# Attention with a bilinear gate on one core: first projections begun on column halves, queries stored before the keys are loaded, last unit summed in one bank

## The chip, the core and the metric

The kernel runs on one core of one Trainium2 chip. The core has five engines with a queue each: TensorE (PE for its matmuls, PEld for its weight loads), VectorE (DVE), ScalarE (ACT), GpSimd (POOL) and SyncE (SP), which here issues every DMA. The engines work at the same time and wait for each other through semaphores. SBUF is the on-chip memory, PSUM the eight banks (128 x 512 float32 each) into which TensorE writes. The metric is the device time of one execution in microseconds (us). Three executions of the kernel before took 1708.01, 1708.64 and 1712.07 us; the median is 1708.64 us.

## The reference

x is 2048 tokens of 512. Its layer norm xn feeds an attention of 32 heads of 16 and a bilinear gate of width 1792; the result is x + attention * silu(gate).

```
xn = (x - mean(x)) / sqrt(var(x) + 1e-5)
q, k, v = split(xn @ wqkv)                       # 32 heads of 16
p = softmax(q @ k.T * 16 ** -0.5)
s = (p @ v).reshape(2048, 512) @ wo
g = silu(((xn @ w_gate) * (xn @ w_up)) @ w_down)
out = x + s * g
```

All arrays are float32. The kernel keeps the accuracy by splitting an operand into a high part (hi), rounded to the matmul's input format, and a low part (lo), the rest; a product is hi*hi + hi*lo + lo*hi, three matmuls.

## The kernel before, in words

The 2048 tokens are 16 tiles of 128, four tiles to a chunk (`c` 0 to 3). The 32 heads are 8 groups of four; a group with one chunk of queries is a unit, so there are 32 units, and a unit walks over the 16 key tiles in 16 rounds. In a round four matmuls `t` (line 639, one for each head) give transposed scores, ACT takes their exponentials `e` (line 641), and `pv` (line 652) multiplies them with the values; two rounds are one block of `pv`. The scores are also computed the other way round (`s`, line 617) to take row maxima on DVE (`mx`, line 619), ahead of the exponentials. The gate's matmuls (`u`, `g`, `y`) and the output projection (`z`) are put between the matmuls of the attention by a filler, so that PE always has work.

The order of the instructions on PE, ACT, DVE and POOL is the order of the program. SP's early part (to round 18) is held to the program's order too; after that a scheduler places SP's DMAs by its own estimate of when each is ready. Each queue is worked through in order, so an instruction that waits holds back all behind it on its engine.

**The start (`early`, lines 714 to 802).** Tiles of x are loaded. The tiles 0 to 3 go through one chain of layer norm: `ln_stats` on DVE for each tile, one square root on ACT for all four (`ln_root`), five small DVE operations (`ln_scale`), then `ln_apply`: tiles 1 and 3 on DVE, 0 and 2 on ACT. `ln_turn` transposes a tile on PE (`xT`) and rounds it into `fh` (hi of chunk 0; DVE for the odd, ACT for the even tiles), `ln_low` forms `fl` on DVE. Then PE projects: `k(0)` (matmuls `p`, 12 of 512 columns: four with the weights' hi `w1h`, four with their lo `w1l`, four with `fl`), `q(0)` in the same way with `w0h` and `w0l`, then values `v`. POOL makes these weights' parts in the order w1h, w1l, w0h, w0l. A table `at` says in front of which of the 252 steps that follow the later tiles are normalised, turned and scored: the first scores stand at step 66, the first that need keys of chunk 1 at step 104.

**The way through DRAM.** A projected chunk leaves PSUM as `hl` (ACT the hi, DVE or POOL the lo), is stored by SP to DRAM (`KD` for keys, `QD` for queries, line 342) and loaded again in the shape of the scores (`ks`, `qs`; `load_k`, `load_q`). SP's order at the start is: store keys 0, load keys 0, store queries 0, load queries 0, then the same for chunk 1.

**The last unit.** Unit 31 has eight blocks. Each block's `pv` goes into one of the three PSUM banks with the tag `st`, which `t` uses in turn as well; the first block is copied into an SBUF tile `acc` by ACT (line 658), the next six are added to it by DVE (line 660). The scores are finished by then, and the banks with the tag `s` have only two users left, two of the output projection's four sums.

**The end (`last_heads`, `final`, `end`).** The last block is added to `acc` in two column halves, each half is transposed, divided by its sum of exponentials and transposed back on DVE; ACT rounds it to `th`, POOL forms the rest `tl`. `final` multiplies both with the last four heads' rows of `wo` (`wrh`, `wrl`): three matmuls for each of four token tiles. `end` multiplies by the gate on DVE, adds x (tiles 0 and 2 on POOL, 1 and 3 on DVE, tile 3 in halves) and stores the tile; here tile means one of the last four, 12 to 15.

## Time and profile before

| | |
|---|---|
| median of three executions | 1708.64 us (1708.01 to 1712.07) |
| the profiled execution's own time | 1709.17 us |
| its span | 1707.0 us |
| PE busy | 1695.4 us, 99% |
| DVE busy | 1441.9 us, 84% |
| ACT busy | 1307.8 us, 77% |
| POOL busy | 872.2 us, 51% |

The profile is of one execution. A row of its timeline has the start and the length in us, the engine, the line, the operation, output<-input by the program's tile names, the shape and the count; what stands in brackets is the idle time of that engine just before and what ended it. A row with a count joins instructions that follow each other. Matmuls overlap: the recorded length of one is longer than the step to the next. SP's rows are the issue of DMAs, not their transfer.

### The profile page before, as it was taken

What the parts mean: (1) busy time and instruction counts of PE and PEld (TensorE: products, weight loads), DVE (VectorE), ACT (ScalarE), POOL (GpSimd) and SP (SyncE); (2) the same over time, 40 slices, a digit from 0 to 9 for tenths busy, and PEclk for the clock granted to TensorE, in tenths of its full rate; (3) what the DMA queues carried; (4) which work ended last, traced back from release to release, by engine and by line L of the source; (5) the groups of instructions that cost most, each with busy time, mean ns of one, the idle gap of its engine ahead of it and who ended that gap; (6) DMA issues with size and microseconds to landing.
All of it is one profiled execution on the core that took longest, in us unless ns stands there. A gap on an engine that the chain in (4) does not pass through costs nothing.

```text
span 1707.0 us, 34993 instructions
## 1 busy us (share of the span) xinstructions
PE 1695.4 (99%) x13570; PEld 1042.1 (61%) x13570; DVE 1441.9 (84%) x2492; ACT 1307.8 (77%) x2565; POOL 872.2 (51%) x873
## 2 busy tenths in 40 slices
PE   8999999999999999999999999999999999999998
PEld 6666656666566666666656665666666566665654
DVE  6888888888888888888888888888888888898953
ACT  6357778777787778778777887877778787777874
POOL 5315545762644647446354572663647536446650
PEclk9999999999999999999999999999999999999999
DMA  6317623620241312412115220330225112111362
GB/s 210 109 48 216 242 104 127 151 66 20 64 91 36 100 60 66 91 45 60 32 52 134 66 72 24 85 79 27 58 83 126 55 36 71 29 54 43 118 187 79
DMA packets 117379, 145.79 MB, mean 85 GB/s; under 512 B 12637, under 2 KB 74333, under 8 KB 114525
## 3 DMA queue, kind: packets, MB, share of 16 engines
q1 hardware_dynamic: 117212, 143.55, 29.3%
q8 instruction: 107, 1.75, 0.4%
q14 instruction: 60, 0.48, 0.1%
HBM read 95.94 MB, written 47.45 MB: 84 GB/s over the span
## 4 chain that ended last, share of the span: by engine, by line
PE 96%; DVE 1%; DMA 1%; issue 0%; POOL 0%; ACT 0%; SPq 0%; POOLq 0%
PE pv L652 28%; PE t L639 19%; PE s L617 12%; PE g L292 6%; PE g L296 5%; PE y L292 5%; PE y L296 5%; PE u L292 5%; PE u L296 4%; PE p L292 3%; PE v L273 2%; PE p L296 2%; PE z L292 2%; PE z L296 1%; DVE mx L619 0%
## 5 line engine op out<-in xcount | busy, mean ns | idle before, releaser
L619 DVE TENSOR_REDUCE mx<-s 128x1 f32<-128x512 f32 x2048 | 1255.0, 681 | 210.4 <-PE s L617 169.0
L641 ACT ACTIVATE e<-t 128x512 f32<-128x512 f32 x2048 | 1101.4, 601 | 96.2 <-PE pv L652 46.5
L639 PE MATMUL t<-qs,ks 50*128 50x512 f32 x2048 | 782.1, 407 | 0.0
L617 PE MATMUL s<-ks,qs 48*128 48x512 f32 x2048 | 767.7, 409 | 0.9 <-DMA ks<-KD 0.4
L63 POOL TENSOR_TENSOR acc<-acc,part 128x512 f32<-128x512 f32 x214 | 278.8, 1303 | 583.8 <-ACT part L663 583.5
L639 PEld LDWEIGHTS t<-qs,ks 50*128 50x128 f32 x2048 | 359.2, 185 | 268.4 <-issue 110.2
L652 PE MATMUL pv<-e,V 128*32 128x512 f32 x4096 | 492.5, 598 | 0.0
L617 PEld LDWEIGHTS s<-ks,qs 48*128 48x128 f32 x2048 | 351.2, 185 | 28.4 <-issue 5.7
L663 ACT ACTIVATE part<-pv 128x512 f32<-128x512 f32 x214 | 128.1, 599 | 204.2 <-PE pv L652 204.2
L652 PEld LDWEIGHTS pv<-e,V 128*32 128x32 f32 x4096 | 107.1, 109 | 242.2 <-issue 220.0
L292 PE MATMUL u<-fh,w0h 64*128 64x512 f32 x224 | 90.5, 404 | 0.0
L296 PE MATMUL g<-fh,w1h 64*128 64x512 f32 x224 | 90.4, 404 | 0.0
L296 PE MATMUL y<-dh,hh 64*128 64x512 f32 x224 | 89.5, 400 | 0.0
L292 PE MATMUL y<-dh,hh 64*128 64x512 f32 x224 | 89.1, 398 | 0.0
L296 PE MATMUL u<-fh,w0l 64*128 64x512 f32 x224 | 88.2, 394 | 0.0
L296 PE MATMUL g<-fl,w1h 64*128 64x512 f32 x224 | 88.1, 393 | 0.0
L292 PE MATMUL u<-fh,w0l 64*128 64x512 f32 x224 | 88.1, 393 | 0.0
L292 PE MATMUL g<-fl,w1h 64*128 64x512 f32 x224 | 88.0, 393 | 0.0
L296 PE MATMUL g<-fh,w1l 64*128 64x512 f32 x224 | 87.9, 392 | 0.0
L292 PE MATMUL g<-fh,w1h 64*128 64x512 f32 x224 | 87.9, 392 | 0.0
L296 PE MATMUL u<-fl,w0h 64*128 64x512 f32 x224 | 87.9, 392 | 0.0
L292 PE MATMUL y<-dl,hh 64*128 64x512 f32 x224 | 87.8, 392 | 0.0
(273 smaller groups left out, 2973.0 us busy)
## 6 DMA issues: line engine op xcount, KB each, us to landing
w1r<-in_wg_dram SPq DMA_DIRECT2D x56, 256.0 KB
w0r<-in_wu_dram SPq DMA_DIRECT2D x56, 256.0 KB
wdr<-in_wd_dram SPq DMA_DIRECT2D x56, 256.0 KB
qs<-QD SPq DMA_DIRECT2D x64, 192.0 KB
ks<-KD SPq DMA_DIRECT2D x12, 768.0 KB
KD<-hl SPq DMA_DIRECT2D x16, 512.0 KB
QD<-hl SPq DMA_DIRECT2D x16, 512.0 KB
OD<-acc SPq DMA_DIRECT2D x31, 256.0 KB
```

What stands on the lines that cost most here:

```text
L63: got = getattr(self.engine, name)(*args, **kw)
L273: nc.tensor.matmul(o, l(d), r(d), start=k == d == 0, stop=k == 2 and d == ND - 1)
L292: nc.tensor.matmul(outs[k], l[LOWER], r[LOWER], start=k == 0 and n == 0, stop=(stop or k == 0) and n == len(low) - 1, skip_group_check=k == 1)
L296: nc.tensor.matmul(outs[1 - k], l[UPPER], r[UPPER], start=k == 0 and m == 0, stop=(stop or k == 0) and m == len(high) - 1, skip_group_chec ...
L617: nc.tensor.matmul(o, QS[i][b:b + KB, pr, t * P:(t + 1) * P], k[b:b + KB, pr, kc * 512:(kc + 1) * 512], start=True, stop=True)
L619: nc.vector.tensor_reduce(MX[i][:, j, t, kc:kc + 1], o, axis=AX.X, op=OP.max)
L639: nc.tensor.matmul(o, k[b:b + KR, pr, kt * P:(kt + 1) * P], QS[i][b:b + KR, pr], start=True, stop=True)
L641: nc.scalar.activation(e, o, AF.Exp, scale=DH ** -0.5)
L652: nc.tensor.matmul(o[32 * j:32 * j + 32], V[:, kt, h0:h0 + 32], es[j], start=n == 0, stop=n == len(todo) - 1)
L663: nc.scalar.activation(part, o, AF.Copy)
```

## The change

In the start, the four tiles are normalised in two chains, tiles 0 and 1 first and 2 and 3 after them, each with its own square root and small operations; tile 1 is now normalised and rounded by ACT. When tiles 0 and 1 are turned, the first four matmuls of `k(0)` run on the columns 0 to 255 alone (tile `hf`), those of `q(0)` (tile `hx`) after tiles 3 and 2 are turned; `full` then does the columns 256 to 511 of these four and the other eight whole. POOL makes both hi parts of the weights first, and the lo parts after them. Keys 0 are loaded after queries 0 are stored. The table `at` moves statistics and normalisations of later tiles by some steps.

PE from its first instruction to the values' projection (xT is a turned tile, its number the tile's; p1 and p0, hf and hx are the key and query projections). Before:

```order
L737 MATMUL warm_199<-acc_127 128x512
L250 MATMUL xT1_227<-ident_129,ks1_135 128x128 x4
L250 MATMUL xT0_233<-ident_129,ks1_135 128x128 x4
L250 MATMUL xT3_239<-ident_129,ks1_135 128x128 x4
L250 MATMUL xT2_245<-ident_129,ks1_135 128x128 x4
L737 MATMUL warm_251<-acc_127 128x512
L273 MATMUL p1_0_0_288<-fh_151,w1h_257 128x512 x4
L273 MATMUL p1_0_0_288<-fh_151,w1l_258 128x512 x4
L273 MATMUL p1_0_0_288<-fl_155,w1h_257 128x512 x4
L273 MATMUL p0_0_0_317<-fh_151,w0h_261 128x512 x4
L273 MATMUL p0_0_0_317<-fh_151,w0l_262 128x512 x4
L273 MATMUL p0_0_0_317<-fl_155,w0h_261 128x512 x4
```

The same place on PE now:

```order
L251 MATMUL xT0_235<-ident_129,ks1_135 128x128 x4
L251 MATMUL xT1_241<-ident_129,ks1_135 128x128 x4
L748 MATMUL warm_249<-acc_127 128x512
L775 MATMUL hf_257<-fh_151,w1h_251 128x256 x4
L251 MATMUL xT3_263<-ident_129,ks1_135 128x128 x4
L251 MATMUL xT2_269<-ident_129,ks1_135 128x128 x4
L775 MATMUL hx_275<-fh_151,w0h_254 128x256 x4
L275 MATMUL hf_257<-fh_151,w1h_251 128x256 x4
L275 MATMUL hf_257<-fh_151,w1l_252 128x512 x4
L275 MATMUL hf_257<-fl_155,w1h_251 128x512 x4
L275 MATMUL hx_275<-fh_151,w0h_254 128x256 x4
L275 MATMUL hx_275<-fh_151,w0l_255 128x512 x4
```

Eight half-width matmuls stand ahead of the point at which all four tiles are turned and rounded; two turned tiles stand between them.

SP, the first stores and loads of keys and queries. Before:

```order
L63 DMA KD0_0_60<-hl_310 128x1024
L63 DMA KD0_0_60<-hl_310 128x512
L63 DMA ks0_134<-KD0_0_60 48x2x512 x2
L63 DMA QD0_0_67<-hl_341 128x1024
L63 DMA QD0_0_67<-hl_341 128x512
L63 DMA qs_346<-QD0_0_67 48x2x512 x2
```

The same place on SP now:

```order
L63 DMA KD0_0_60<-hl_329 128x1024
L63 DMA KD0_0_60<-hl_329 128x512
L63 DMA QD0_0_67<-hl_356 128x1024
L63 DMA QD0_0_67<-hl_356 128x512
L63 DMA ks0_134<-KD0_0_60 48x2x512 x2
L63 DMA qs_363<-QD0_0_67 48x2x512 x2
```

The load of keys 0 moved behind the store of queries 0; what follows stands as it did.

In the last unit all eight blocks of `pv` add up in one bank `last` with the tag `s`; the copy by ACT and the adds by DVE are gone, and `t` has the three `st` banks to itself. `last_heads` transposes straight from that bank. The hi and the lo of a head are laid side by side in the 32 rows that a head's block has (`both`, made by POOL), so one transposition on DVE and one copy on ACT serve both, and `final` needs two matmuls a tile, eight in all. For that the rows of `wrh` are copied into the unused rows beside them by four small DMAs on SP. In `end` tile 0 and tile 1 are added on POOL, tile 2 on DVE, and tile 3 in halves on DVE. The program's text stores tile 1 between the halves of tile 3.

SP, the last stores (y is the tile that holds the last four token tiles; the brackets name the engines waited for). Before:

```order
L63 DMA out_0_dram<-dl_24577 128x512 [waits DMAHW6_49,DMAHW2_49,DVE_49]
L63 DMA out_0_dram<-dl_24577 128x512 [waits DVE_49]
L63 DMA out_0_dram<-y_19450 128x512 [waits Pool_49]
L63 DMA out_0_dram<-y_19450 128x512 [waits DMAHW1_49,DVE_49]
L63 DMA out_0_dram<-y_19450 128x512 [waits Pool_49]
L63 DMA out_0_dram<-y_19450 128x256 [waits DVE_49] x2
```

The same place on SP now:

```order
L63 DMA out_0_dram<-dl_24595 128x512 [waits DMAHW6_49,DMAHW2_49,DVE_49]
L63 DMA out_0_dram<-dl_24595 128x512 [waits DVE_49]
L63 DMA out_0_dram<-y_19468 128x512 [waits Pool_49]
L63 DMA out_0_dram<-y_19468 128x512 [waits DMAHW5_49,Pool_49]
L63 DMA out_0_dram<-y_19468 128x512 [waits DVE_49]
L63 DMA out_0_dram<-y_19468 128x256 [waits DVE_49] x2
```

As built, the stores stand in the order tile 0, 1, 2, then the halves of 3: the scheduler has put tile 1's, which waits for POOL, ahead of tile 2's and of both halves of tile 3's.

The diff, cut to its core:

```diff
@@ split_raw @@
-    def split_raw(name, raw, after=None):
         hi, lo = [wtile(name + n) for n in "hl"]
         pool.tensor_copy(hi, raw)
-        low = pool.tensor_tensor(lo, raw, hi, op=OP.subtract)
-        if after is not None:
+        def rest():
+            low = pool.tensor_tensor(lo, raw, hi, op=OP.subtract)
             tc.add_manual_dep(low.ins, after.ins.name, BEHIND, reason="keeps the port free for the layer norm")
-        return hi, lo
+        return (hi, lo), rest
@@ full @@
+            part = slice(256 if begun and k == 0 else 0, 512)
             for d in range(ND):
-                nc.tensor.matmul(o, l(d), r(d), start=k == d == 0, stop=k == 2 and d == ND - 1)
+                nc.tensor.matmul(o[:, part], l(d), r(d)[:, part], start=k == d == 0 and not begun, stop=k == 2 and d == ND - 1,
+                                 skip_group_check=begun)
@@ end @@
-            pool.tensor_tensor(yt, yt, xt, op=OP.add)
-        dma(out[tt * P:(tt + 1) * P], yt)
+        (nc.vector if t == 2 else pool).tensor_tensor(yt, yt, xt, op=OP.add)
+        if t != 1:
+            dma(out[tt * P:(tt + 1) * P], yt)
@@ ending @@
+        for j in range(0, P, 32):
+            dmar(wrh[j + DH:j + 32], wrh[j:j + DH])
...
+        def final(t):
+            for n, r in enumerate((wrh, wrl)):
+                nc.tensor.matmul(banks[t], fst["t"][:, t * P:(t + 1) * P], r, start=False, stop=n == 1,
+                                 skip_group_check=True)
@@ block @@
-        o = psum("st", f"pv{i}")
+        whole = i == NU - 1
+        if whole and todo[0][1] == 0:
+            fst["last"] = psum("s", "last")
+        o = fst["last"] if whole else psum("st", f"pv{i}")
@@ last_heads @@
-            nc.vector.tensor_tensor(acc[:, c], o[:, c], acc[:, c], op=OP.add)
-            nc.vector.transpose(flat, acc[:, c])
+            nc.vector.transpose(tr[:, b].rearrange(flat), o[:, c])
             nc.vector.reciprocal(rc[:, b], tr[:, b, DH:DH + 1])
             nc.vector.tensor_tensor(tr[:, b, 0:DH], tr[:, b, 0:DH], rc[:, b].to_broadcast([P, 8, DH]), op=OP.mult)
-            nc.vector.transpose(acc[:, c], flat)
-            nc.scalar.activation(th[:, c], acc[:, c], AF.Copy)
-            pool.tensor_tensor(tl[:, c], acc[:, c], th[:, c], op=OP.subtract)
+            pool.tensor_copy(both[:, b, 0:DH], tr[:, b, 0:DH])
+            pool.tensor_tensor(both[:, b, DH:32], tr[:, b, 0:DH], both[:, b, 0:DH], op=OP.subtract)
+        for h in range(2):
+            c, b = slice(256 * h, 256 * h + 256), slice(8 * h, 8 * h + 8)
+            nc.vector.transpose(back[:, c], both[:, b].rearrange(flat).bitcast(F32))
+            nc.scalar.activation(fst["t"][:, c], back[:, c], AF.Copy)
@@ early @@
-        first = (0, 1, 2, 3)
-        ln_open(first)
-        for tt in first:
-            ln_stats(tt)
-        ln_root(first)
-        ln_scale(first)
-        port = ln_apply(1)
...
+        first = (0, 1), (2, 3)
...
+        ln_root(first[0])
+        ln_scale(first[0])
+        ln_apply(0)
+        ln_apply(1)
+        ln_stats(2)
+        ln_stats(3)
+        ln_root(first[1])
+        ln_scale(first[1])
+        ln_turn(0)
+        ln_turn(1)
+        port = ln_apply(3)
+        ln_apply(2)
         warm(1)
...
+        def first_half(w, tag):
+            half[tag] = o = psum(tag, f"h{tag}")
+            for d in range(ND):
+                nc.tensor.matmul(o[:, 0:256], w[0][:, d], xh[0][:, d, 0:256], start=d == 0, stop=False,
+                                 skip_group_check=True)
+        first_half(wk, "f")
+        ln_low(0)
+        ln_turn(3)
+        ln_turn(2)
+        first_half(wq, "x")
...
         def q(c):
-            yield from qk_proj(wq, 0, 0, c, "f" if c else "x")
+            yield from qk_proj(wq, 0, 0, c, "f" if c else "x", None if c else half["x"])
+            if not c:
+                load_k(0, [c])
             load_q(c)
...
-        for tts, n, root, scale in ((tuple(range(4, 8)), 0, 13, 25), (tuple(range(8, NT)), 16, 52, 53)):
+        for tts, n, root, scale in ((tuple(range(4, 8)), 0, 13, 16), (tuple(range(8, NT)), 16, 52, 53)):
```

More of the change, by code (lines that the diff above doesn't have):

```diff
@@ L305, in qk_weights, with qk_proj @@
         return split(f"w{which}", wqkv[:, c0:c0 + P])
-    def qk_proj(w, m, which, c, tag):
+    def qk_proj(w, m, which, c, tag, o=None):
         wh, wl = w
-        o = psum(tag, f"p{which}_{m}_{c}")
+        begun = o is not None
+        o = o if begun else psum(tag, f"p{which}_{m}_{c}")
         hi, lo = [lambda d, w=w: w[:, d] for w in (wh, wl)]
-        yield from full(o, ((hi, lambda d: xh[c][:, d]), (lo, lambda d: xh[c][:, d]), (hi, lambda d: xl[c][:, d])))
+        yield from full(o, ((hi, lambda d: xh[c][:, d]), (lo, lambda d: xh[c][:, d]), (hi, lambda d: xl[c][:, d])), begun)
         hl = qp.tile([P, 2, D], F32R, name="hl", bufs=HBUFS)
@@ L569, in ending @@
             yield
-        for todo in (0, 1), (2, 3):
-            final(todo, (0, 1))
-            final(todo, (2,))
+        for t in range(4):
+            final(t)
+        for t in range(4):
+            end(NC - 1, t, banks[t], fst["y"][:, t], xr[:, t])
     NU = NG * NC
@@ L652, in block @@
                 nc.tensor.matmul(o[32 * j:32 * j + 32], V[:, kt, h0:h0 + 32], es[j],
-                                 start=n == 0, stop=n == len(todo) - 1)
-        if todo[-1][1] == NT - 1 and i == NU - 1:
-            last_heads(o)
+                                 start=(kt if whole else n) == 0, stop=kt == NT - 1 if whole else n == len(todo) - 1,
+                                 skip_group_check=whole)
+        if whole:
+            if todo[-1][1] == NT - 1:
+                last_heads(o)
         elif todo[0][1] == 0:
@@ L760, in k @@
         def k(c):
-            yield from qk_proj(wk, 0, 1, c, "f")
-            load_k(0, [c])
+            yield from qk_proj(wk, 0, 1, c, "f", None if c else half["f"])
+            if c:
+                load_k(0, [c])
         def q(c):
-            yield from qk_proj(wq, 0, 0, c, "f" if c else "x")
+            yield from qk_proj(wq, 0, 0, c, "f" if c else "x", None if c else half["x"])
+            if not c:
+                load_k(0, [c])
             load_q(c)
```

61 lines of the change are left out of this document (28 added, 33 removed).

## The prediction, made before the changed kernel was run

> **What bounds the kernel now.** I read the page first: busy time, then the share of PE.
>
> ```profile
> span 1707.0 us, 34993 instructions
> PE 1695.4 (99%) x13570; PEld 1042.1 (61%) x13570; DVE 1441.9 (84%) x2492; ACT 1307.8 (77%) x2565; POOL 872.2 (51%) x873
> ```
>
> PE is busy for 99% of the span, so a change counts where PE waits or works for nothing: at the start, in the last unit, and behind the last matmul. What is won at the start is kept to the end, because the stream of matmuls behind it is the same. The profiled execution took 1709.17 us, 2.2 us more than its span; it lies 0.53 us above the median of 1708.64 us.
>
> The timeline of the start comes next.
>
> ```profile
> 4.96 0.18 DVE L205 BATCH_NORM_AGGREGATE mv<-st 128x2 f32<-128x6 f32 x1
> 5.90 0.69 DVE L204 BATCH_NORM_STATS2 st<-ks 128x6 f32<-128x512 f32 x1 [0.76 <-DMA ks<-in_x_dram]
> 7.38 0.61 POOL L63 CAST w1h<-w1r 128x512 fp32r<-128x512 f32 x1 [5.19 <-DMA w1r<-in_wqkv_dram]
> 7.64 0.30 ACT L208 ACTIVATE r<-mv,eps 128x4 f32<-128x4 f32 x1 [5.41 <-DVE mv L205]
> 7.97 0.18 DVE L214 RECIPROCAL r<-r 128x4 f32<-128x4 f32 x1 [0.36 <-ACT r L208]
> 8.97 1.52 ACT L235 ACTIVATE ks<-ks,mr,e 128x512 f32<-128x512 f32 x2 [1.03 <-DVE mr L220]
> 8.97 1.00 DVE L234 TENSOR_SCALAR ks<-ks,e,mr 128x512 f32<-128x512 f32 x2
> 9.66 1.94 PE L250 MATMUL xT<-ident,ks 128*128 128x128 f32 x16 [2.70 <-DVE ks L234]
> 11.63 0.60 ACT L260 ACTIVATE fh<-xT 128x512 fp32r<-128x512 f32 x1 [0.27 <-PE xT L250]
> 11.80 2.47 DVE L265 TENSOR_TENSOR fl<-xT,fh 128x512 fp32r<-128x512 f32 x4
> 12.33 1.16 PE L273 MATMUL p<-fh,w1h 128*128 128x512 f32 x4
> 18.11 2.03 PE L273 MATMUL v<-e,fh 128*128 128x512 f32 x8
> ```
>
> Statistics of four tiles, a square root (7.64), five small operations (7.97 to 8.97, 1.0 us), normalising, 16 transpositions, rounding: only at 12.33 does PE begin the key projection, and the values follow at 18.11. The last row gives the step of a 512-column matmul: (2.03 - 0.40)/7 = 0.23 us, where 0.40 is the recorded length of one. The 16 transpositions have a step of 1.94/16 = 0.12.
>
> The next rows show PE waiting again, and the way through DRAM.
>
> ```profile
> 18.08 0.81 SPq L63 DMA_DIRECT2D KD<-hl  x2
> 21.38 0.80 SPq L63 DMA_DIRECT2D ks<-KD  x2
> 22.01 0.66 PE L250 MATMUL xT<-ident,ks 128*128 128x128 f32 x4 [0.47 <-ACT ks L235]
> 22.28 0.86 SPq L63 DMA_DIRECT2D QD<-hl  x2
> 27.41 0.79 SPq L63 DMA_DIRECT2D qs<-QD  x2
> 30.56 0.47 PE L617 MATMUL s<-ks,qs 48*128 48x512 f32 x1
> 31.29 0.71 PE L617 MATMUL s<-ks,qs 48*128 48x512 f32 x3 [0.26 <-DMA qs<-QD]
> 35.73 0.59 ACT L313 ACTIVATE hl<-p 128x512 fp32r<-128x512 f32 x1
> 38.49 0.81 SPq L63 DMA_DIRECT2D KD<-hl  x2
> 45.81 0.46 PE L617 MATMUL s<-ks,qs 48*128 48x512 f32 x1
> 46.71 0.70 PE L617 MATMUL s<-ks,qs 48*128 48x512 f32 x3 [0.43 <-DMA ks<-KD]
> ```
>
> PE waits three times: at 22.01 for tile 4 (ACT's normalising), at 31.29 for the queries, at 46.71 for the keys of chunk 1. A store lands 3.3 us (18.08 to 21.38) or 5.1 us (22.28 to 27.41, with the keys' load beside it) after its issue, a load is used 3.9 us (27.41 to 31.29) after its own; for keys of chunk 1 store and load take 8.2 us together (38.49 to 46.71).
>
> **The start, step by step.** *First chain.* Tile 1's statistics end at 5.14; square root to 5.5, five small operations to 6.5. The first chain's root no longer waits for tile 2, which arrives at 5.90. ACT then normalises tiles 0 and 1 (1.52) to 8.0. *Second chain.* DVE does the statistics of tiles 2 and 3 behind the small operations, 2 x (0.69 + 0.18) at most, to 8.2; root to 8.5, small operations to 9.5; tile 3 on DVE (1.00/2) to 10.0, tile 2 on ACT to 10.3. The added root and five operations (1.3 us) so lie beside ACT's work on the first two tiles, which ACT rounds from 8.5 to 9.6.
>
> *Half-width matmuls.* They start at 9.7, once tile 1 is rounded; w1h is there (7.38 + 0.61), w0h is made next. No row shows a 256-column matmul. The bounds are the transposition's 0.12 (128 columns with a weight load each) and 0.23; half of 0.23 is 0.12, and the transpositions show that a weight load fits into such a step, so I take 0.12. Then: hf to 10.2, two turned tiles (8 x 0.12) to 11.1, hx to 11.6. ACT rounds tile 2 (0.60) from 11.3 to 11.9; the other halves begin at 12.0: 4 x 0.12 + 4 x 0.23 to 13.4. fl is ready: DVE has one low part before tile 3's rounding and three (0.60 each, from 2.47/4) after it, to 13.2. Keys end at 14.3, queries 0.48 + 1.84 later at 16.6, against 18.11: **1.5 us**. POOL's lo parts, moved behind w0h, start after 10.0 and are needed at 12.5 and 14.8.
>
> *Tile 4.* DVE's statistics of tiles 4 to 7 now start at 13.2 and end at 16.4, hl of the keys 17.0, small operations 18.0 (moved ahead of the queries' hl), ACT's tile 4 at 18.8. PE wants it at 19.9 (1.5 and the wait before 22.01), so the wait goes: 0.47 printed, and since a record ends 0.17 after the next matmul could have begun (0.40 - 0.23), **0.64 us**.
>
> *Queries in front of keys on SP.* Store of keys at 17.0, of queries at 18.65 (hl behind the small operations, 0.6), landed by 23.8 even at 5.1; their load is used by 27.7. The keys' load, which the store is now ahead of, is issued between 20.3 and 22.1 and lands by 26.0. PE comes to the first scores at 30.56 - 1.5 - 0.64 = 28.4. Both are early by 0.7 us or more. The wait was 0.73 from 30.56 to 31.29 less one score's 0.21: **0.52 us**.
>
> *Keys of chunk 1.* ACT made their hl at 35.73, behind four normalisations (0.76 each, from 8.97's row). Two of the four now stand behind it (1.5 us), and the rest comes some 2.1 us earlier, as PE does: hl near 32.1, store 2.8 later as before, at 34.9, use at 43.1. PE is there at 45.81 - 2.14 - 0.52 + 0.21 = 43.4. The wait of 0.90 - 0.23 goes: **0.67 us**, with only 0.3 us to spare. Late next are tiles 10 and 11, whose normalising moved: ACT ends tile 11's at 35.5, when PE wants it; I take nothing for that and keep 0.3.
>
> Sum of the start: 1.5 + 0.64 + 0.52 + 0.67 = **3.3 us**, between 2.0 and 3.6.
>
> **The last unit.** The waits of the window 1640 to 1697 and the first matmuls behind a block:
>
> ```profile
> 1684.06 3.81 ACT L641 ACTIVATE e<-t 128x512 f32<-128x512 f32 x7 [0.70 <-PE t L639]
> 1684.10 0.39 PE L296 MATMUL z<-fl,hl 64*128 64x512 f32 x1
> 1684.41 0.50 PE L639 MATMUL t<-qs,ks 50*128 50x512 f32 x1
> 1684.75 0.39 PE L292 MATMUL z<-fh,dh 64*128 64x512 f32 x1
> PEld t L639 <- DVE acc L660: 2.5, 7, 0.4
> ```
>
> The third `t` behind a block waits until DVE has read the block's bank. From 1684.10 to 1684.75 two steps take 0.65 instead of 0.46: 0.19 lost, most of it because no weights are loaded ahead during a wait. Of the seven waits listed two belong to unit 30; with the one for ACT's copy of the first block six go: 6 x 0.19 = **1.1 us**. Above, the idle time as printed gives 6 x 0.35 = 2.1. Below, nothing, if `t` then waits for ACT at the same place; ACT's seven exponentials take 3.81 us and it sat idle for 0.70 before them, so I stay near the row. DVE's six adds and ACT's copy are off the path. The four copies of `wrh` rows in SP's queue stand ahead of loads for chunk 2's output that are used only in the unit's last blocks: nothing.
>
> **The end.**
>
> ```profile
> 1653.27 2.14 DVE L492 TENSOR_TENSOR dl<-dl 128x512 f32<-128x512 f32 x2
> 1653.79 1.07 POOL L63 CAST hl<-w1r 128x512 fp32r<-128x512 f32 x1
> 1678.31 1.28 DVE L492 TENSOR_TENSOR hh<-hh 128x512 f32<-128x512 f32 x2
> 1694.95 0.42 DVE L699 TENSOR_TENSOR acc<-pv,acc 128x256 f32<-128x256 f32 x1 [3.44 <-PE pv L652]
> 1698.74 1.28 PE L561 MATMUL z<-hl,g 128*128 128x512 f32 x4
> 1699.17 0.69 DVE L484 TENSOR_TENSOR y<-z,y 128x512 f32<-128x512 f32 x1 [0.38 <-PE z L561]
> 1701.87 1.26 POOL L63 TENSOR_TENSOR y<-y,hh 128x512 f32<-128x512 f32 x1 [0.56 <-DVE y L484]
> 1703.09 0.42 DVE L480 TENSOR_TENSOR y<-z,hh 128x256 f32<-128x256 f32 x1
> L63 SPq DMA_DIRECT2D out_dram<-y x5: 332/377/472, 1701.3 to 1704.0; - x5
> GB/s 0 0 0 0 0 0 0 0 0 0 72 338 389 399 369 399 379 277 0 31 348 358 420 307 343 338 343 133 0 0 0 0 0 0 0 0 0 0 0 0
> ```
>
> `last_heads` now: per half transposition, reciprocal, product on DVE, 1.05 us each from 1694.95; POOL's rounding and rest of 128 columns, 0.7 between 0.5 (the rows' 0.61 and 1.26 for 512 scaled down) and 1.9 (not scaled); back through DVE and ACT: first half at 1698.0, second at 1698.8. PE does tile 0's two matmuls at 1698.05; DVE's first product follows 0.43 behind the last of them, as 1699.17 follows 1698.74: at 1698.7, **0.47 us earlier**. DVE's work behind it is the same eight operations as before (4.3 us, 1699.17 to 1703.51).
>
> But tile 2's add on DVE reads two SBUF tiles while POOL adds tiles 0 and 1. Two such adds took 2.14 us at 1653.27 with POOL at work and 1.28 at 1678.31 with POOL idle; POOL's rounding took 1.07 instead of 0.61. So DVE loses 0.4 and ends at 1703.4, and POOL's second add, done at 1702.0 without that, ends about 1702.65.
>
> As SP stands, the stores of tile 2 and of tile 3's halves wait behind tile 1's, which waits for that add. With 0.38 for an issue: 1702.65, 1703.05, 1703.4, 1703.8; before, the last began at 1704.0. The bytes say the other sign: at some 350 GB/s (the slices at full rate) 768 KB behind 1702.65 end 0.2 us later than 512 KB behind 1703.13 (1701.87 + 1.26) did. I take **0**, between 0.8 earlier (no collision) and 0.6 later.
>
> The Trainium skill's page "SBUF — State Buffer", section "SBUF: two separate sides", says that the shared port pair is an exclusive lock which the loser waits for during the whole instruction. By it tile 2's add could wait for all of a POOL add (1.26), and the end would come 0.4 us later than I take; the two rows above show 0.43 an add, and I go by them.
>
> **Sum.** 3.3 + 1.1 + 0 = 4.4 us: 1709.17 becomes 1704.8 for the profiled execution, and 1708.64 becomes **1704.2 us** for the median, 0.26% less. What a measurement of this kernel can tell from no change is about 0.3%, 5.1 us: the line is at 1703.5.
>
> **Rivals.**
> - *The end pays.* If DVE and POOL do not collide, tile 1's store goes at 1702.0 and the end is 0.8 earlier; with the start at 3.6: 1708.64 - 5.5 = 1703.1. For it: at 1701.87 POOL's add ran in 1.26 beside DVE, though DVE then read a PSUM bank. Chance 0.30.
> - *Half-width matmuls cost as much as whole ones* (0.23): queries end at 17.9 and the start gains 2.0. 1705.5, chance 0.08. Against it: the transpositions' 0.12.
> - *The waits come back*: keys of chunk 1 or the first queries late after all, `t` waiting for ACT. 1.5 + 0.64 is left: 1706.5, chance 0.12. For it: 0.3 us to spare.
> - *Slower.* The mechanism is SP's order: keys 0 wait behind the queries' store, that for DVE's hl, that for five small operations, that for ACT's root, that for the statistics of tiles 4 to 7, loaded from 5.89 on. Whatever delays that chain now delays keys and queries together. Each us beyond 0.7 costs one; it decides at 0.7 + 4.4 = 5.1 us, and 10.2 us make the kernel 0.3% slower, near 1714. No row speaks for so much. Chance 0.13, for this and what I don't see.
>
> The Trainium skill's page "TensorE: Matmul & The Clock Gate", section "LDWEIGHTS (loading the stationary operand)", gives columns/1.2 ns, 107 ns for 128 columns. Were that not hidden behind the matmul, a half would be an estimated 0.22 us and the second rival true; the trace's step of 0.23 for 512 columns with a load each speaks for hiding.
>
> **How the numbers follow.** Forecast 0.37 (its own range 1703.3 to 1705.4, a quarter of it below 1703.5), rivals 0.30, 0.08, 0.12, 0.13. Faster: 0.30 + 0.10 = 0.40. Same: 0.27 + 0.08 + 0.12 = 0.47. Slower: 0.13. The range runs from 1702.4 (start 3.6, last unit 1.8, end 0.8) to 1706.8 (waits back, end 0.3 later) and leaves out the slower rival and the edges.
>
> **What the changed profile would show.** The second half of hf near 12.0 and the values near 16.6; no idle ahead of tile 4, the first scores near 28.4 and step 104 near 43 without a wait; no wait of `t` for DVE in the last 45 us; tile 2's add on DVE near 1.1 us instead of 0.65; last store's issue about 9 us after the last `pv` as before (1704.0 - 1694.8). I am wrong if scores wait again, if a half-width step is 0.2, or if the shift at step 104 is lost later.

## The result, and the profile after

The changed kernel takes 1704.66 us (median of nine executions, 1704.20 to 1705.57) against 1708.64 us, a ratio of 0.9974 with a 95% interval of 0.9964 to 0.9985. The forecast was 1704.2 us in a range of 1702.4 to 1706.8. The profiled execution took 1704.54 us.

The page of the changed kernel, first lines: span, then busy time by engine.

```profile
span 1702.8 us, 35005 instructions
PE 1693.3 (99%) x13574; PEld 1042.9 (61%) x13574; DVE 1437.5 (84%) x2487; ACT 1307.8 (77%) x2567; POOL 873.5 (51%) x875
```

PE worked 2.1 us less than before (1695.4) and waited 2.1 us less (span less PE: 9.5 after 11.6). The timeline of the start follows, with the marks that the prediction named (lines 251, 275, 621, 643 answer to 250, 273, 617, 639 of before).

```profile
9.76 0.71 PE L775 MATMUL hf<-fh,w1h 128*128 128x256 f32 x4
10.30 1.06 PE L251 MATMUL xT<-ident,ks 128*128 128x128 f32 x8
12.05 0.74 PE L275 MATMUL hf<-fh,w1h 128*128 128x256 f32 x4 [0.21 <-ACT fh L261]
16.86 2.03 PE L275 MATMUL v<-e,fh 128*128 128x512 f32 x8
17.26 0.80 SPq L63 DMA_DIRECT2D KD<-hl  x2
19.16 0.82 SPq L63 DMA_DIRECT2D QD<-hl  x2
20.12 0.60 PE L251 MATMUL xT<-ident,ks 128*128 128x128 f32 x4
28.51 0.73 PE L621 MATMUL s<-ks,qs 48*128 48x512 f32 x4
30.38 0.66 PE L251 MATMUL xT<-ident,V 128*128 128x128 f32 x4
31.57 0.73 PE L275 MATMUL p<-xh,w0h 128*128 128x512 f32 x2
32.90 0.72 PE L621 MATMUL s<-ks,qs 48*128 48x512 f32 x4
35.14 0.81 SPq L63 DMA_DIRECT2D KD<-hl  x2
43.53 0.73 PE L621 MATMUL s<-ks,qs 48*128 48x512 f32 x4
96.12 0.50 PE L643 MATMUL t<-qs,ks 50*128 50x512 f32 x1
```

The second half of `hf` starts at 12.05, the values at 16.86 (before 18.11); tile 4, the first scores and the scores of step 104 have no bracket, so PE didn't wait there. The lead over the kernel before can be followed row by row: 1.25 us at the values, 1.89 at tile 4 (22.01), 2.57 at the second of the first scores (31.29 against 28.51 + 0.21), 2.20 at the next scores (before they began at 35.10), 2.97 at step 104 (46.71 against 43.53 + 0.21), 3.16 at the first `t`, which was at 99.28. It grows at each wait that went, and falls once, between 28.5 and 32.9. There two small waits are new, for tile 8 and ahead of the queries' projection; PE loses 0.16 and 0.22 us in them. From the start of the two matmuls ahead to what follows it takes 0.63 us (29.75 to 30.38) and 0.78 us (30.79 to 31.57), and in the kernel before 0.47 us (32.49 to 32.96) and 0.56 us (33.31 to 33.87) at the same places.

The last block of the last two units, before and after (`last` is the new bank), shows what the last unit gave:

```profile
1645.94 1.92 PE L652 MATMUL pv<-e,V 128*32 128x512 f32 x16
1692.91 1.92 PE L652 MATMUL pv<-e,V 128*32 128x512 f32 x16
```

```profile
1642.75 1.92 PE L659 MATMUL pv<-e,V 128*32 128x512 f32 x16
1688.67 1.92 PE L659 MATMUL last<-e,V 128*32 128x512 f32 x16
```

The lead is 3.19 us at the end of unit 30 and 4.24 at the last `pv`: the last unit gave 1.05 us. The wait of `t` for DVE's sums, seven times and 2.5 us in all in the kernel before, is left once, in unit 30:

```profile
PEld t L643 <- DVE acc L669: 0.3, 1, 0.3
```

The end:

```profile
1694.42 1.89 DVE L489 TENSOR_TENSOR y<-z,y 128x512 f32<-128x512 f32 x3 [0.25 <-PE z L567]
1695.19 2.96 POOL L63 TENSOR_TENSOR y<-y,hh 128x512 f32<-128x512 f32 x2 [1.50 <-DVE y L489]
1696.34 0.69 DVE L493 TENSOR_TENSOR y<-y,hh 128x512 f32<-128x512 f32 x1
1696.50 3.58 SPq L63 DMA_DIRECT2D out_dram<-y  x5
```

The bandwidth by windows (start:end, length, PE, PEld, DVE, ACT, POOL busy with counts, PE clock, DMA share, GB/s):

```profile
1698.50:1699.00 0.50, 0.00 (x0) 0.00 (x0) 0.26 (x1) 0.00 (x0) 0.00 (x0) 0.68 0.05 12
1701.00:1701.50 0.50, 0.00 (x0) 0.00 (x0) 0.00 (x0) 0.00 (x0) 0.00 (x0) 0.50 0.57 193
```

DVE's first product follows the last `pv` by 5.75 us, 0.51 less than before (1699.17 - 1692.91 = 6.26). But from the last `pv` to the end of the span it takes 14.1 us in both kernels. The gain of VectorE is lost between its work and the stores: the DMA engines are nearly idle ahead of 1699.0 (12 GB/s) and then have 768 KB to move, which keeps them busy past 1701.0.

### The profile page after: what moved, and what is told of

It is laid out like the page before. It is cut to its first block, busy times and chain, and to the rows that moved or that the text cites. A ratio compares the mean times of both kernels' runs of the same rounds, so it can differ in the third digit from the quotient of the medians.

```text
span 1702.8 us, 35005 instructions
## 1 busy us (share of the span) xinstructions
PE 1693.3 (99%) x13574; PEld 1042.9 (61%) x13574; DVE 1437.5 (84%) x2487; ACT 1307.8 (77%) x2567; POOL 873.5 (51%) x875
## 4 chain that ended last, share of the span: by engine, by line
PE 98%; DVE 1%; ACT 0%; DMA 0%; POOL 0%; issue 0%; ACTq 0%
PE pv L659 27%; PE t L643 19%; PE s L621 12%; PE g L295 6%; PE y L295 5%; PE u L295 5%; PE g L299 5%; PE y L299 4%; PE u L299 3%; PE p L295 3%; PE v L275 2%; PE z L295 2%; PE p L299 2%; PE last L659 1%; PE z L299 1%; PE p L275 1%
## 5 line engine op out<-in xcount | busy, mean ns | idle before, releaser
L659 PE MATMUL pv<-e,V 128*32 128x512 f32 x3968 | 477.1, 598 | 0.0
L299 PE MATMUL g<-fh,w1h 64*128 64x512 f32 x224 | 90.6, 404 | 0.0
L295 PE MATMUL g<-fh,w1l 64*128 64x512 f32 x224 | 87.9, 392 | 0.0
L299 PE MATMUL g<-fh,w1l 64*128 64x512 f32 x224 | 87.9, 392 | 0.0
L295 PE MATMUL y<-dh,hl 64*128 64x512 f32 x224 | 87.8, 392 | 0.0
```

The source lines that it names most:

```text
L295: nc.tensor.matmul(outs[k], l[LOWER], r[LOWER], start=k == 0 and n == 0, stop=(stop or k == 0) and n == len(low) - 1, skip_group_check=k == 1)
L299: nc.tensor.matmul(outs[1 - k], l[UPPER], r[UPPER], start=k == 0 and m == 0, stop=(stop or k == 0) and m == len(high) - 1, skip_group_chec ...
L659: nc.tensor.matmul(o[32 * j:32 * j + 32], V[:, kt, h0:h0 + 32], es[j], start=(kt if whole else n) == 0, stop=kt == NT - 1 if whole else n ...
```

## The experiments

Each kernel was timed in alternation with the kernel before, which took 1708.99 us beside the first set (`start_only`, `tail_only`, `one_bank_old_end`, `stores_in_order`), 1709.01 beside the second (`changed_again`, `keys_first`, `no_halves`, `norm_earlier`) and 1709.15 beside the third (`keys_first_fed`, `no_halves_fed`, `old_table`, `add2_on_gpsimd`). Differences below are against these, or against the changed kernel as timed in the second set, 1704.91 us.

**The two ends of the change apart.** `start_only` is the changed kernel with the old functions `block`, `last_heads`, `final` and `end`, and without the copies of `wrh` rows:

```diff
-        o = fst["last"] if whole else psum("st", f"pv{i}")
+        o = psum("st", f"pv{i}")
...
-        for t in range(4):
-            final(t)
+        for todo in (0, 1), (2, 3):
+            final(todo, (0, 1))
+            final(todo, (2,))
```

`tail_only` has only these from the change, and the old `early`, `full` and `qk_proj`:

```diff
-        first = (0, 1), (2, 3)
+        first = (0, 1, 2, 3)
...
-        first_half(wk, "f")
```

> The start of the change alone (two chains of layer norm, column halves, the table of steps, the queries' store in front of the keys' load), with the last unit and the end of the kernel before. By my theory the start's shift of 3.2 us (the first t at 96.12 us against 99.28 us in the two traces) is kept to the end and nothing else moves: 1708.64 - 3.2 = 1705.4 us, within 0.4. The rival, that part of the shift comes from or is lost in the last unit, gives less than 1705.0 or more than 1706.0.

> The last unit and the end of the change alone, with the start of the kernel before. By my theory the last unit gives 1.05 us (3.19 of lead at its start, 4.24 at its last pv in the trace of after) and the end nothing: 1707.6 us, within 0.4, and the two halves of the change add up to 4.25 us. The rival, that the two do not add, shows as a sum of both gains that differs from 4.0 by more than 0.6.

`start_only` took 1705.87 us, 3.12 less than the kernel before (ratio 0.9980, 0.9972 to 0.9989), `tail_only` 1707.79 us, 1.20 less (0.9994, 0.9985 to 1.0003). The sum, 4.32 us, agrees with the change's 4.1 in the second set: within this noise the two halves add up. The interval of `tail_only` includes no change at all, so what the last unit is worth is better read from the traces: there it gave 0.99 us in `tail_only` and 1.05 us in the next run, as in the changed kernel.

**One bank, old end.** The kernel before, and in it:

```diff
-        o = psum("st", f"pv{i}")
+        o = fst["last"] if whole else psum("st", f"pv{i}")
...
-            nc.vector.tensor_tensor(acc[:, c], o[:, c], acc[:, c], op=OP.add)
-            nc.vector.transpose(flat, acc[:, c])
+            nc.vector.transpose(flat, o[:, c])
```

> The kernel before with only the last unit's sums kept in one bank; the rounding of the last heads, the six matmuls, the products and the stores stay those of before, less the addition of the last block (0.42 us a half), which the bank makes needless. My theory: the last unit gives its 1.05 us here too, and the end is shorter by 0.4 to 0.8, as the addition lay on its path and the stores of before wait for nothing else: 1707.0 us (1706.7 to 1707.3), so 0.4 to 0.8 better than the last unit and the end of the change together. The rival, that the rewritten end is worth as much as the addition it drops, or more: 1707.6 or above.

It took 1707.44 us, 1.55 less than before (0.9990, 0.9981 to 0.9999). That lies between theory and rival. The trace shows more:

```profile
1691.18 1.92 PE L655 MATMUL last<-e,V 128*32 128x512 f32 x16
1695.66 0.39 PE L292 MATMUL z<-fh,w0l 64*128 64x512 f32 x1
1697.01 1.08 PE L561 MATMUL z<-hl,g 128*128 128x512 f32 x4
1697.44 0.69 DVE L484 TENSOR_TENSOR y<-z,y 128x512 f32<-128x512 f32 x1 [0.81 <-PE z L561]
```

From the last `pv` to the first product it takes 6.26 us, exactly as before: in the old end the addition was not on the path. PE is still busy with the open sums of chunk 3 until about 1695.9, and tile 0's third and last final matmul is the fifth behind them, at 1697.01; the product follows 0.43 later. So the dropped addition alone buys nothing, and my expectation of 0.4 to 0.8 at the end fell. In the changed kernel tile 0 is through after two matmuls, and its product comes 0.51 us earlier, although the first of the two starts later behind the last `pv` (1693.66 - 1688.67 = 4.99 against 1695.97 - 1691.18 = 4.79). It waits for ACT's rounding there and no longer for PE, so the addition could count in the new end; no run has the new end with the addition. The 0.35 us between this kernel and `tail_only` are there in the traces before the last unit, at the end of unit 30 (1645.26 against 1645.59), up to which both run the program of before. The first `t` came at 98.54 and 98.80 us, against 99.28 in the trace of the kernel before, so the unchanged start itself varies by that much.

**The stores in the written order.** The changed kernel, and ahead of the last stores:

```diff
         while "t" not in fst:
             yield
+        Tied.on = True
```

which holds SP to the order of the program.

> The changed kernel with the last five stores issued in the order in which they are written in the code: tiles 0, 2, first half of 3, tile 1, second half of 3. My theory: the end's gain on VectorE (0.54 us) is lost because the stores of tile 2 and of tile 3's first half, whose data are there at 1697.03 and 1697.83 us, stand behind tile 1's, which waits for GpSimd's second addition until 1698.15; the DMA engines are idle for the us before 1699.0. In the new order 384 KB less move after 1699.0 and the last issue comes right behind the last operation at 1698.76 instead of 1699.6: 0.5 to 0.8 us faster than after, 1703.9 to 1704.2 us. The rival, that the end hangs on the last store's own latency behind VectorE's last operation or on the rate of the DMA engines, whatever the order: within 0.2 us of after.

```profile
1688.88 1.92 PE L660 MATMUL last<-e,V 128*32 128x512 f32 x16
1696.71 2.70 SPq L63 DMA_DIRECT2D out_dram<-y  x5
1698.50:1699.00 0.50, 0.00 (x0) 0.00 (x0) 0.44 (x2) 0.00 (x0) 0.00 (x0) 1.00 0.98 356
1700.50:1701.00 0.50, 0.00 (x0) 0.00 (x0) 0.00 (x0) 0.00 (x0) 0.00 (x0) 0.87 0.08 23
```

It took 1703.96 us, 5.03 less than the kernel before (0.9969, 0.9958 to 0.9981), where the change gave 4.1 in the second set. By the two medians of the changed kernel (1704.66 and 1704.91) that is 0.7 to 0.9 us better, at the upper end of the theory or a little over it. The issues of the five stores span 2.70 instead of 3.58 us, in the window from 1698.5 the bytes move at 356 GB/s, where the changed kernel had 12, they are through by 1701.0 (23 GB/s in the last window), and the span ends 13.1 us behind the last `pv` (1702.0 - 1688.88) instead of 14.1. The order in SP's queue ate the end's gain.

**Tile 2's addition on GpSimd**, in addition to the ordered stores (one execution, 1705.75 us):

```diff
-        (nc.vector if t == 2 else pool).tensor_tensor(yt, yt, xt, op=OP.add)
+        pool.tensor_tensor(yt, yt, xt, op=OP.add)
```

> The changed kernel with the stores in the written order and tile 2's last addition on GpSimd, behind those of tiles 0 and 1, instead of on VectorE. My theory: GpSimd's second addition took 1.72 us because VectorE's addition of two SBUF tiles (0.69 us) ran beside it; without that each of the three takes 1.26 to 1.30. VectorE ends 0.6 us earlier, at about 1697.9 us, but tile 2's store waits for GpSimd until 1699.2 (1695.4 + 3 x 1.28), so the span ends 0.2 to 0.6 us later than with VectorE's addition. The rival, that the store of tile 0, which reads SBUF meanwhile, slows the second addition: 1.7 us again.

The groups by line, for the changed kernel and then for this one:

```profile
L63 POOL TENSOR_TENSOR y<-y,hh 128x512 f32<-128x512 f32 x2 | 3.0, 1500 | 1.5 <-DVE y L489 1.5
```

```profile
L63 POOL TENSOR_TENSOR y<-y,hh 128x512 f32<-128x512 f32 x3 | 3.7, 1266 | 1.5 <-DVE y L489 1.5
1697.05 4.24 SPq L63 DMA_DIRECT2D out_dram<-y  x5
```

Three additions take 1266 ns each here; with VectorE's addition beside them two took 1500 on average, so the second took about 1.73. The collision is real, and here GpSimd pays for it, not VectorE (0.69 us in the row at 1696.34). The store of tile 0 isn't the cause. VectorE doesn't always come off free. In the run with one bank and the old end its product of 128 columns took 0.29 us for the first half and 0.80 us for the second, beside an operation of GpSimd:

```profile
1695.27 0.73 POOL L63 TENSOR_TENSOR g<-acc,g 128x256 fp32r<-128x256 f32 x1 [36.95 <-ACT g L707]
1695.35 0.80 DVE L705 TENSOR_TENSOR tr<-tr,rc 128x128 f32<-128x128 f32 x1
```

In both cases the operation that began second lost: GpSimd's second addition 0.09 us behind VectorE's (1696.43 against 1696.34), VectorE's product 0.08 us behind GpSimd's. The time I gave was too small: the span ends 14.8 us behind the last `pv` (1704.0 - 1689.22), 1.7 later than with VectorE's addition, since in the written order tile 2's store holds back all three behind it, and it now waits for the third addition.

**The changed kernel again, as a base.**

> The changed kernel itself, as the base for the kernels run beside it on the same chip: 4.0 to 4.4 us faster than before, as measured already. No theory differs here.

1704.91 us, 4.10 less than the kernel before (0.9975, 0.9965 to 0.9985).

**Keys first on SP.** The load of keys 0 back in front of the queries' store:

```diff
-            if c:
-                load_k(0, [c])
+            load_k(0, [c])
...
-            if not c:
-                load_k(0, [c])
```

> The changed kernel with SyncE's old order at the start: the load of the keys of chunk 0 back in front of the queries' store. My theory: the load waits for the keys' store to land (issue 17.26, landed by 21.15 us in the trace of after) and holds the queries' store from 19.16 to about 22.0; that lands 3.9 to 5.1 us later, the queries' load is used 3.9 us after its issue, so at 29.8 to 31.0, while PE is at the second score at 28.7: a wait of 1.1 to 2.3 us at the first scores, all of it kept to the end: 1.1 to 2.3 us slower than the changed kernel beside it. In the kernel before, the swap looked worth only its wait of 0.52 us, since PE came later there. The rival, that the new wait is 0.5 us as before or that a wait behind it is covered by it: 0 to 0.6 us slower.

It took 1709.67 us, 4.8 more than the changed kernel, and as much as the kernel before (ratio 1.000, 0.9991 to 1.0009). Theory and rival were both far too low. SP and PE:

```profile
27.62 0.80 SPq L63 DMA_DIRECT2D qs<-QD  x2
30.80 2.03 PE L621 MATMUL s<-ks,qs 48*128 48x512 f32 x4 [2.43 <-DMA qs<-QD]
38.05 0.73 PE L621 MATMUL s<-ks,qs 48*128 48x512 f32 x4
```

The wait lies just above what I forecast (1.1 to 2.3 us): the scores begin at 30.80 instead of 28.42 us, 2.38 late. But the four scores then take 2.03 us instead of 0.73, and the next scores begin 7.25 us later instead of 4.40 (28.42 to 32.82 in the run beside it). PE alone in windows (length, busy with count, granted clock, DMA share, GB/s):

```profile
26.00:28.00 2.00, 2.00 (x11) 1.00 0.04 14
31.00:32.00 1.00, 0.92 (x3) 0.50 0.00 0
37.00:38.00 1.00, 1.00 (x6) 0.81 0.00 0
```

Behind the pause the granted clock is 0.50 until about 37.4 us (the mean of 0.81 in the last window is 0.38 us at half), so for some 6.6 us of work, with no DMA traffic beside it, and that costs another 2.85 us. The first `t` is at 101.27 us, 5.23 behind the changed kernel's 96.04.

**The same, with PE kept at work through the wait.**

```diff
+            if n == 66:
+                warm(10)
```

> The kernel with the keys' load in front of the queries' store, with ten matmuls on zeros (10 x 0.23 us) put on PE ahead of the first scores, where it waited 2.7 us; their result is not used. My theory: of the 4.8 us that this order cost, the wait itself is 2.4 to 2.7, and the rest is TensorE's granted clock, which stood at 0.50 from 31 to 37.2 us behind the wait. With PE fed through the wait the clock stays at 1.00: 2.3 to 2.9 us slower than the changed kernel (1707.2 to 1707.8 us by 1704.9), and about 2.2 faster than without the ten matmuls. The rival, that the slow matmuls come from what runs beside them (DMA traffic, other engines' PSUM access) and not from the pause: the four scores take 2.0 us again and the time is 1709 to 1710 us.

```profile
28.36 8.74 PE L748 MATMUL warm<-acc 128*128 128x512 f32 x20
37.03 0.74 PE L621 MATMUL s<-ks,qs 48*128 48x512 f32 x4
40.85 0.73 PE L621 MATMUL s<-ks,qs 48*128 48x512 f32 x4
31.00:32.00 1.00, 1.00 (x4) 1.00 0.00 0
```

1713.17 us: the ten matmuls were mis-sized. They multiply float32 tiles, are recorded as 20, and take 8.74 us instead of the 2.3 that I worked out from the projections' 0.23; so the time says nothing on the wait. The rows behind them do: the four scores take 0.74 us, and the next scores follow in 3.82 us, not 7.25. With no pause ahead of them the same matmuls run at full clock. The granted clock is 1.00 in every window from 24 to 39 us, also between 31 and 37 us (the last line), which speaks against what goes on beside PE at that time as the cause. That, and the granted clock of 0.50 above, carry the reading that the pause is what slowed them.

**Without column halves**, two chains kept:

```diff
-        first_half(wk, "f")
+        half.update(f=None, x=None)
...
-        first_half(wq, "x")
```

> The changed kernel without the column halves: two chains of layer norm as they are, but the key and query projections begin at full width once all four tiles are turned. My theory: eight 256-column matmuls (8 x 0.115 = 0.92 us) that ran while PE waited for tiles 2 and 3 come on top behind 12.0 us; nothing behind them waits: 0.9 us slower than the changed kernel beside it (0.7 to 1.1). Rival one, that the two chains alone carry the gain, since other waits behind absorb the 0.9: within 0.3. Rival two, that the halves carry nearly all of the 1.5 us: 1.3 or more.

```profile
11.95 1.17 PE L275 MATMUL p<-fh,w1h 128*128 128x512 f32 x4 [0.73 <-ACT fh L261]
```

The profiled execution took 1705.76 us, 0.9 more than the changed kernel's median, with values at 17.51 (0.74 later than the 16.77 beside it) and the first `t` at 96.79 (0.75 later): the forecast of 0.9 holds there. But the median of its eleven executions is 1707.16 us, 2.25 more, and they range from 1705.20 to 1708.99 us; three of the four above 1707.7 have a mean granted clock of 0.998, the others 0.999. Ahead of the projection PE pauses for 0.73 us (the bracket above), where the changed kernel pauses for 0.21. So the same kernel again, with matmuls in that pause:

```diff
         ln_turn(2)
+        warm(3)
```

> The kernel without the column halves, with three matmuls on zeros (3 x 0.23 = 0.69 us) on PE in the pause behind the turned tiles (11.2 to 11.95 us). My theory: the median of 1707.16 us without them mixes executions at 0.9 us above the changed kernel, as forecast and as the profile has it, with others in which the clock dropped behind the pauses of the start; fed, the runs come together at 1705.6 to 1706.0 us with a spread of under 1.2 us, and the halves proper are worth 0.9. The rival, that the spread has another cause: median 1706.5 or more, spread of 3 us as before.

1707.58 us, from 1707.35 to 1708.63. These three matmuls too were four times as long as I took them for, and the first `t` comes at 98.90 us, 2.1 later than without them: so the time is no measure of the halves. What the run does show is the spread, 1.3 us instead of 3.8, with no execution under a clock of 0.999. So feeding PE ends the spread, which fits a clock that sometimes drops behind the pauses; no trace of such an execution was taken, and this stays argued. The halves are worth 0.75 us at the first `t` of the trace, 0.9 by its span, and 2.3 by the median.

**The old table of steps** in the changed kernel (statistics, normalisations, small operations):

```diff
-(1, (0, 2, 4, 6), (25, 25, 25, 25), ...), (2, (26, 26, 28, 30), (60, 60, 73, 75), ...
+(1, (0, 2, 4, 6), (26, 26, 26, 26), ...), (2, (16, 20, 26, 27), (60, 60, 62, 62), ...
...
-(tuple(range(4, 8)), 0, 13, 16)
+(tuple(range(4, 8)), 0, 13, 25)
```

> The changed kernel with the old table of steps: small operations of tiles 4 to 7 behind the rest of the queries, four normalisations in front of the rounding of chunk 1's keys, statistics where they were. My theory: tile 4 is ready 0.6 us later, at about 20.2 us, which PE wants at 20.1: 0 to 0.4; chunk 1's keys are stored 1.5 us later, at 36.6 us instead of 35.1, and used 8.2 us behind that, at 44.8, where PE comes at 43.5 to 43.9: a wait of 0.9 to 1.3 us. Together 0.9 to 1.7 us slower than the changed kernel, 1705.8 to 1706.6 us; more only if PE's clock drops behind that wait. The rival, that the table only follows the rest and carries nothing: within 0.4 of it.

```profile
18.55 0.66 DVE L323 TENSOR_TENSOR hl<-hx,hl 128x512 fp32r<-128x512 f32 x1
20.11 1.52 ACT L236 ACTIVATE ks<-ks,mr,e 128x512 f32<-128x512 f32 x2 [2.66 <-DVE mr L221]
20.98 0.66 PE L251 MATMUL xT<-ident,ks 128*128 128x128 f32 x4 [0.90 <-ACT ks L236]
37.45 0.81 SPq L63 DMA_DIRECT2D KD<-hl  x2
45.34 0.71 PE L621 MATMUL s<-ks,qs 48*128 48x512 f32 x3 [0.38 <-DMA ks<-KD]
```

1707.34 us, 2.4 more than the changed kernel in the second set (0.9989 of the kernel before, 0.9980 to 0.9998). Both waits are back. At step 104 it is 0.65 us (44.48 to 45.34, less a score), under my 0.9 to 1.3. At tile 4 it is 1.07 (19.45 plus two matmuls is 19.91; PE goes on at 20.98), over my 0 to 0.4: ACT's normalisation starts at 20.11, not 0.6 but 1.5 us later than the 18.57 of the changed kernel, because in the old table two statistics of tiles 8 and 9 also stand ahead on VectorE. Together these are 1.7 us, and the first `t` of this trace comes 1.85 us later (97.89 against 96.04); the rest of the 2.4 isn't accounted for. The rival fell: the table carries a large part of the gain.

**A shorter way to tiles 8 and 9**, with the ordered stores:

```diff
-        if tts[0] < 8:
-            on = nc.vector.scalar_tensor_tensor
+        on = nc.vector.scalar_tensor_tensor
...
-(26, 26, 28, 30), (60, 60, 73, 75)
+(26, 26, 28, 30), (61, 61, 73, 75)
```

> The changed kernel with the last five stores in the written order, and with the chain in front of tiles 8 and 9 shortened: the small operations of tiles 8 to 15 on VectorE instead of GpSimd (seven of them took 27.57 to 29.48 us behind GpSimd's low parts), and the normalisations of tiles 8 and 9 one step later, behind ScalarE's copy of the third block of values. My theory: the two new waits of the changed kernel, for tile 8 at 30.38 and for that copy at 31.57 us, cost PE 0.2 and 0.3 us; both go, and the lead is kept: 0.5 us at the start and 0.5 to 1.0 at the end, so 1.0 to 1.5 us faster than the changed kernel beside it. The rival, that the start's 0.5 us come back as a wait for the keys of chunk 1 at step 104: 0.5 to 1.0 us faster, and scores that wait at about 43 us.

```profile
42.78 0.73 PE L613 MATMUL s<-ks,qs 48*128 48x512 f32 x4
95.36 0.50 PE L635 MATMUL t<-qs,ks 50*128 50x512 f32 x1
1688.44 1.92 PE L651 MATMUL last<-e,V 128*32 128x512 f32 x16
```

In the trace both new waits are gone, no scores wait at 42.78, and the first `t` comes 0.68 us before that of the changed kernel beside it (96.04). At the last `pv` 0.43 is left of it (1688.44 against 1688.87), and the span of 1701.5 is 1.4 shorter than the 1702.9 there. The median is 1704.01 us, 0.9 less than the changed kernel (0.9970 of the kernel before, 0.9959 to 0.9981): no more than the ordered stores alone gave. Whether the 0.4 to 0.7 us of the start reach the median is open. These two kernels, at 1703.96 and 1704.01 us, are the fastest here.

## Why the prediction was right, point by point

**The start, 3.3 forecast, 3.16 in the trace, 3.12 alone.** Its marks came as given: second half of `hf` 12.05 (12.0), values 16.86 (16.6), first scores 28.51 (28.4), store of chunk 1's keys 35.14 (34.9), step 104 at 43.53 (43) without a wait. Half-width matmuls cost half: the four of `hf` begin at 9.76 and the next transposition at 10.30, so a step is at most 0.135 us; that rival fell. The terms fit less well than their sum. The first projections gave 1.25 us of the 1.5. "I take nothing for that" was wrong for the normalisations that moved: two new waits of 0.38 us together came, though at tile 8 and behind the copy of values, not at tiles 10 and 11. The waits that went gave 0.64 at tile 4, as priced, 0.68 instead of 0.52 at the queries, and 0.93 instead of 0.67 at the keys of chunk 1, counted to the scores that follow them (50.50 before, 47.37 now). Some 0.6 us too much and 0.4 too little nearly cancel: that the sum came out so near is luck in part.

**What the parts are worth was wrong, not the sum.** I priced the swap on SP at the 0.52 us of the wait that I saw. Taken out of the changed kernel it costs 4.8 us, of which 2.85 in the trace are the halved clock behind the wait; the old table costs 2.4, the halves 0.9 by the trace. These come to more than the 3.2 us that all of them give: each brings PE forward to the next thing that is late, so a part that shows a wait of 0.5 us in the kernel before can hold the whole lead in the kernel after. With the old order on SP the queries came at 30.8 us in the changed kernel and at 31.3 in the kernel before, wherever PE was by then.

**The rival "Slower" had the right place and the wrong price.** The delay that it names, keys and queries late together in the new order, did not come. But another wait at the same scores, with the keys first, shows what one costs. "Each us beyond 0.7 costs one" holds for a wait that leaves the clock alone. In the run with the keys first 2.38 us of wait cost 5.23 at the first `t`. By my price the kernel could have become no faster than before only from 4.4 us of lateness behind the 0.7; in truth 2.4 us of wait were enough.

**The last unit, 1.1 forecast, 1.05 in the trace.** The waits of `t` went as forecast, and none for ScalarE took their place at a cost.

**The end, 0 forecast, 0 in the trace** (14.13 us behind the last `pv`, 14.09 before). VectorE's first product came 0.51 us earlier (0.47 forecast), and the order of the stores as built took it back, as worked out; the run with the ordered stores shows that. The rival "the end pays" fell by that order, and by the collision, which did delay tile 1's store; with the order mended the kernel took 1703.96 us, still above the rival's 1703.1. The step that failed is who pays in the collision: I let both lose, VectorE 0.4 us and GpSimd's second addition 0.65. VectorE lost nothing (0.69 us for tile 2's addition, where I had given 1.1 as a sign), and GpSimd's second addition lost 0.46 (1.73 instead of 1.27). The forecast of 0 didn't hang on VectorE's loss: as the stores stand, those of tiles 2 and 3 wait behind tile 1's, whose data GpSimd had ready only at 1698.15. The Trainium skill's page "SBUF — State Buffer", section "SBUF: two separate sides", has the loser wait for the whole instruction of the other. The trace agrees with it in part: GpSimd's second addition began at 1696.43, while VectorE's ran until 1697.03, and of these 0.60 us it lost 0.46. I had applied the rule with the wrong loser.

The sum, 4.4, stands against 4.2 us between the two spans and 4.0 between the medians. Of the rivals, "the waits come back" was true of no wait that it named.

## What to carry to other kernels

When waits stand in a chain, price each at its row for the sum, but don't read that as the part's worth: take one part out of the finished kernel and look again. A long wait of PE can cost more than its length: here one of 2.4 us cost 5.2, because the matmuls behind it ran at half clock, so look at the granted clock behind it. When engines at the end are rebalanced, read the order of the stores as built: one store that waits holds back all behind it, and here it was worth 0.7 to 0.9 us, nearly as much as the whole last unit.

## What the hardware showed that I had not expected

- A pause of PE of about 2.6 us (28.2 to 30.8 us) was followed by some 6.6 us of work at a granted clock of 0.50, which cost 2.85 us; pauses of 0.65 and 1.07 us in the run with the old table were not (1.00 in the windows around them). The Trainium skill's page "TensorE: Matmul & The Clock Gate", section "Part 1: The HAM clock gate (the "warmup" mystery)", puts the drop behind an idle window of about 3.4 us, and full speed behind as long a busy one. Here less idle time was enough, and the return took nearly twice that.
- Not every such pause does it. In the kernel before, PE paused for 2.70 us ahead of the first transpositions (the row at 9.66), and the granted clock behind it was 1.00 in the trace. Its executions spread from 1708.04 to 1713.76 us in the second set, and 7 of the 27 have a mean granted clock of 0.998 or less; those of the changed kernel beside it spread from 1704.50 to 1705.84, none below 0.999. So the shorter pauses at the start may also have narrowed the spread; that the long pause made it is argued, not shown.
- A float32 matmul of 512 columns on zeros, recorded as two, took 0.87 us (8.74 / 10), against 0.23 for one in the projections' format.
- VectorE's addition of two SBUF tiles held up GpSimd's, begun 0.09 us later, by 0.46 us, and GpSimd's operation held up VectorE's product, begun 0.08 us later, by 0.5 us; with one of VectorE's operands in PSUM GpSimd's additions kept their 1.27 us.
